# Tail rows as the stationary operand of the first expert product, transposed on TensorE, and a new order of all steps

## The chip, the core and the metric

The kernel runs on one core of a Trainium2 chip. Its engines work side by side, each through its own instructions in order: TensorE (PE: matmuls, with PEld its weight loads), VectorE (DVE), ScalarE (ACT), GpSimd (POOL, which here mostly issues DMAs), SyncE (SP, which issues DMAs). The metric is the device time of one execution in microseconds, lower is better. It is the median over several runs; a separate, profiled execution gives the trace.

## The reference

Attention with a causal window of 64 over 8 batches, 8 heads, 576 positions and head size 64; then a mixture of experts in which each batch, as a whole, is sent to one of 8 experts by the mean of its rows.

```python
scores = scale * np.matmul(q, k.transpose(0, 1, 3, 2))
mask = (rel >= 0) & (rel < window)
...
attn = attn / (np.sum(attn, axis=-1, keepdims=True) + 1e-09)
return np.matmul(attn, v).astype(np.float32)
...
pooled = x.mean(axis=1)
logits = pooled @ w_gate
e_idx = np.argmax(logits, axis=1)
...
h = np.maximum(x[mask] @ w1[e], 0.0)
out[mask] = gate_w[mask, None, None] * (h @ w2[e])
```

Per batch x is 576 x 512, w1 is 512 x 1024 and w2 1024 x 512.

## The kernel before

**Rows.** The 576 positions of a batch are 512 main rows and 64 tail rows. Attention is cut in units: four a batch with two heads each for the main rows, and a fifth for the tail rows of all heads. So unit 5b+i is part i of batch b, and units 4, 9, 14, ... are tails.

**Steps and their order.** The kernel has no loop that sets the order. `OPS`, a table of some 900 words, lists every step, and the words are carried out one after the other; each engine then runs its own instructions in that order and waits on semaphores where data or a buffer isn't ready. A word is a letter, sometimes a letter for the engine or the PSUM pool (a: ACT, d: DVE, m: the pool of the expert chunks, b: the mask is added by PE), and a number. `Q`, `t`, `L`, `W` issue loads on POOL's queue (q and k of a batch, its tail q and k, a piece of v, half of an expert's w1 or w2). `T` transposes q and k of a unit on PE, `U` and `k` copy the results out of PSUM, `S` makes the scores, `E` the exponentials, `K` masks them on DVE, `l` the row sums (spread over partitions by a matmul with ones, into the PSUM tile `lb`), `n` and `R` their Ln and the exponential of its negative on ACT (the reciprocal), `A` the product with v, `X` the scaling, with a sum over rows for the gate. `V` copies v to a second alignment (a shift by 64 partitions). `g j G H I P` work out the gate; `P` makes POOL read the expert's number, on which the addresses of the `W` loads depend.

**Expert chunks.** `c` takes the next chunk of a fixed list: in each batch eight chunks of the first product (128 hidden units by 512 main rows, 8 matmuls each), one for the tail rows, four pairs of half chunks of the second product (one pair for 128 output rows), and one for the tail's second product. `r` evacuates the oldest finished chunk on ACT (`ra`) or DVE (`rd`): a relu with the gate's weight for the first product (L446 on ACT, L448 on DVE), a copy for the second (L482, L487 for the tail). `O` and `o` store a finished output tile through POOL's or SP's queue (L492). `F` would issue filler matmuls; the table before has none.

**The tail's first product (L470).** For each of 8 tiles of 128 hidden units, 4 contraction blocks and 2 halves of 64 columns, the weights are stationary (64 columns) and the 64 tail rows are the moving operand: 64 matmuls a batch. Their result has hidden units on partitions, as the second product needs it.

**Buffers.** PSUM has eight banks: one for transposes (`ps_t`), two for scores (`ps_s`), one for `lb` and one for `av` (`ps_a`), three that expert chunks share with some transposes, scores and av (`ps_m`). V has three buffers, w1 and w2 three slots. POOL's loads and stores have eight completion semaphores in turn, so that each waits for the landing of the one eight before it.

## Time and profile before

| | |
|---|---|
| median of 3 runs | 204.0 us (203.14 to 204.12) |
| span of the profiled execution, first to last instruction | 201.9 us |
| PE busy, share of the span | 183.5 us, 91% |
| ACT, DVE, POOL busy | 131.8, 119.9, 111.0 us |
| read from and written to HBM | 61.88 and 9.44 MB |
| matmuls of the tail's first product (L470) | 512, busy 9.5 us |
| matmuls of the tail's second product (L512) | 128, busy 8.5 us |

The span of the trace and the runs' times are different measurements; what a reading of the trace gives is a difference of spans. PE's busy time counts overlapping matmuls once. The chain of waits follows the work that ended last back from the end; a piece of it on PE is the pace of successive matmuls, while the mean of a group is one matmul's own duration, longer because neighbours overlap. A wait names what came last by the profile.

### The profile page before, as it was taken

The page shows a single profiled execution, that of the slowest core. Times are in us where ns is not written, and L with a number is a line of the kernel's source. Part 1 is how long each engine was busy: PE and PEld are TensorE (multiplying, and loading weights), DVE is VectorE, ACT ScalarE, POOL GpSimd, SP SyncE. Part 2 cuts the span into 40 slices and gives each one's busy share as a digit, 9 for nine tenths or more (in the row PEclk, how much of TensorE's full clock was granted, in tenths as well). Part 3 has the DMA queues.
Part 4 walks back from the last instruction along what each step waited for, and adds up shares of the span by engine and source line. Part 5 has one row for each costly group of instructions (what it writes and reads, how often), then busy time and mean ns, then how long its engine had stood idle before and what let it go on. Part 6 is the DMA issues. An engine that isn't in the chain of part 4 may idle for free.

```text
span 201.9 us, 8105 instructions
## 1 busy us (share of the span) xinstructions
PE 183.5 (91%) x3518; PEld 124.2 (62%) x3522; DVE 119.9 (59%) x347; ACT 131.8 (65%) x247; POOL 111.0 (55%) x158
## 2 busy tenths in 40 slices
PE   0487886899999999999999999999999999999991
PEld 0455564656677756577667666676656666776760
DVE  3527989595477546895877457966494651216410
ACT  2179998876599578977779975757787436321121
POOL 7985939235931593478633552439452716553561
PEclk9999999999999999999999999999999999999998
DMA  6999999999999999999999999999999999999693
GB/s 135 175 188 159 194 162 198 199 198 174 196 201 197 170 198 193 174 201 167 200 206 200 169 195 223 259 208 137 183 237 243 266 254 212 274 212 301 235 325 134
DMA packets 83346, 41.16 MB, mean 204 GB/s; under 512 B 48080, under 2 KB 80976, under 8 KB 83312
## 3 DMA queue, kind: packets, MB, share of 16 engines
q0 software_dynamic: 81936, 39.72, 138.5%
q1 hardware_dynamic: 768, 0.85, 1.3%
q8 instruction: 27, 0.44, 0.8%
q10 hardware_dynamic: 608, 0.08, 0.2%
q14 instruction: 7, 0.06, 0.1%
HBM read 61.88 MB, written 9.44 MB: 353 GB/s over the span
## 4 chain that ended last, share of the span: by engine, by line
PE 77%; DMA 9%; POOL 7%; issue 3%; DVE 2%; ACT 1%; POOLq 0%; DVEq 0%; ACTq 0%
PE ph L461 28%; PE po L503 25%; DMA vw<-in_v_dram 9%; PE tp L225 5%; PE ph L470 4%; PE s L275 4%; PE av L331 3%; PE po L512 3%; PE lb L309 3%; POOL vw L141 2%; POOL km L110 2%; POOL qm L110 1%; POOL out_dram L492 1%; PE gps L392 1%; POOL qkt L133 1%
## 5 line engine op out<-in xcount | busy, mean ns | idle before, releaser
L503 PE MATMUL po<-w2b,hm 128*64 128x512 f16 x512 | 60.1, 379 | 0.0
L461 PE MATMUL ph<-xm,w1b 128*64 128x512 f16 x512 | 60.0, 379 | 0.0
L461 PEld LDWEIGHTS <-w1b 128*64 128x64 f16 x512 | 31.7, 110 | 18.7 <-issue 0.4
L503 PEld LDWEIGHTS <-hm 128*64 128x64 f16 x512 | 30.1, 110 | 19.3
L141 POOL DMA_DIRECT2D vw<-in_v_dram x32 | 28.9, 910 | 13.3 <-DMA w1b<-in_moe_w_dram 4.3
L446 ACT ACTIVATE hm<-ph,gw 128x512 f16<-128x512 f32 x39 | 26.6, 693 | 13.4 <-PE ph L461 13.3
L492 POOL DMA_DIRECT2D out_dram<-ob x31 | 17.2, 557 | 25.0 <-DMA w1b<-in_moe_w_dram 7.0
L351 ACT ACTIVATE ln<-lb 128x512 f32<-128x512 f32 (+1 forms) x40 | 22.5, 563 | 11.8 <-PE lb L309 8.6
L364 DVE CUSTOM_DVE_ANT_0 xm<-av,rl 128x512 f16<-128x512 f32 x32 | 21.6, 686 | 10.4 <-PE av L331 9.5
L482 ACT COPY ob<-po 128x512 f32<-128x512 f32 x18 | 10.6, 586 | 23.6 <-PE po L503 23.6
L448 DVE TENSOR_SCALAR hm<-ph,gw 128x512 f16<-128x512 f32 x25 | 18.7, 748 | 12.1 <-PE ph L461 11.6
L357 ACT ACTIVATE rl<-ln 128x512 f32<-128x512 f32 (+1 forms) x40 | 23.3, 594 | 1.5 <-DVE pool L364 1.3
L225 PE MATMUL tp<-ident,qm 128*64 128x128 bf16 x256 | 13.8, 232 | 7.4 <-DMA qm<-in_q_dram 6.9
L288 ACT ACTIVATE pe<-s 128x1024 f16<-128x1024 f32 x19 | 19.5, 1028 | 1.4 <-PE s L275 0.7
L297 DVE TENSOR_TENSOR pe<-pe,mask 128x1024 f16<-128x1024 f16 x24 | 16.3, 687 | 3.9 <-ACT pe L288 3.1
L252 ACT COPY kT<-tp 128x512 bf16<-128x512 bf16 x19 | 11.2, 597 | 9.0 <-PE tp L225 8.0
L225 PEld LDWEIGHTS <-qm 128*64 128x64 bf16 x256 | 10.7, 118 | 10.0 <-DMA qm<-in_q_dram 6.9
L482 DVE COPY ob<-po 128x512 f32<-128x512 f32 x14 | 9.7, 690 | 10.7 <-PE po L503 10.5
L423 POOL DMA_DIRECT2D w1b<-in_moe_w_dram x16 | 12.6, 785 | 5.9 <-DMA vw<-in_v_dram 2.9
L275 PEld LDWEIGHTS <-kT 64*128 64x128 bf16 x576 | 10.1, 95 | 8.9 <-issue 5.6
L331 PEld LDWEIGHTS <-vw 128*64 128x64 f16 x512 | 12.4, 112 | 4.7 <-issue 1.2
L225 PE MATMUL tp<-ident,km 128*64 128x128 bf16 x256 | 13.9, 231 | 1.4 <-DMA km<-in_k_dram 0.9
(80 smaller groups left out, 267.2 us busy)
## 6 DMA issues: line engine op xcount, KB each, us to landing
w1b<-in_moe_w_dram POOLq DMA_DIRECT2D x16, 512.0 KB, 9.3
w2b<-in_moe_w_dram POOLq DMA_DIRECT2D x16, 512.0 KB, 13.4
out_dram<-ob POOLq DMA_DIRECT2D x31, 256.0 KB, 8.1
vw<-in_v_dram POOLq DMA_DIRECT2D x32, 128.0 KB, 9.0
km<-in_k_dram POOLq DMA_DIRECT2D x7, 512.0 KB, 9.3
qm<-in_q_dram POOLq DMA_DIRECT2D x7, 512.0 KB, 9.0
out_dram<-obt POOLq DMA_DIRECT2D x14, 64.0 KB, 7.7
qkt<-in_q_dram POOLq DMA_DIRECT2D x8, 64.0 KB, 7.6
```

The costliest lines, as they stand in the source:

```text
L141: nc.gpsimd.dma_start(out=vt[:, 2 * J + 1], in_=v[b, :, 128 * J:128 * J + 128].rearrange("h c d -> c h d"))
L225: nc.tensor.transpose(tp[p0:p0 + 64, n, r], t[:, 2 * i + hh, ts(r, 64)], ident)
L288: nc.scalar.activation(out=po, in_=sp[0], func=AF.Exp, scale=scale)
L351: nc.scalar.activation(out=ln, in_=lb[:, 0:n], func=AF.Ln)
L357: nc.scalar.activation(out=rl, in_=lns.pop((b, i)), func=AF.Exp, scale=-1.0)
L364: nc.vector.tensor_tensor_reduce(out=xm[:, i], in0=av.rearrange("q r p -> q (r p)"), in1=rl, scale=1.0, scalar=0.0, op0=ALU.mult, op1=ALU.add,
L446: nc.scalar.activation(out=o, in_=i, func=AF.Relu, scale=g)
L448: nc.vector.tensor_scalar(out=o, in0=i, scalar1=g, scalar2=0.0, op0=ALU.mult, op1=ALU.max)
L461: nc.tensor.matmul(out=ph[64 * c:64 * c + 64], lhsT=w1t[:, kb, ts(2 * ft + c, 64)], rhs=xm[:, kb], start=(kb == 0), stop=(kb == 3), skip_g ...
L482: copy(e)(out=ob, in_=po)
L492: (nc.scalar if n and eng is nc.sync else eng).dma_start(out=dst, in_=src)
L503: nc.tensor.matmul(out=po[64 * c:64 * c + 64], lhsT=hm[:, fb, ts(2 * r + c, 64)], rhs=w2t[:, fb], start=(fb == 0), stop=(fb == 7), skip_gr ...
```

## The change

The 64 tail rows become the stationary operand (`xt`, 64 columns) and half of w1's columns, 512 of them, the moving one: 8 matmuls a batch. The result has rows on partitions (row half c holds hidden units 512c to 512c+511), so after the relu, now into `hs`, eight transposes on PE turn it (step `B`, into a bank of `ps_t` or, with m, `ps_m`), and a copy out of PSUM puts it into `ht` (step `D`, on ACT or DVE). The second product is as before. A 16-bit identity `identh` is copied once, in `tail_mask`. The filler matmul writes 64 partitions instead of 128, and the table uses it once, with 2 matmuls, behind the last chunk.

```diff
     def tail_mask():
+        nc.vector.tensor_copy(out=identh, in_=ident)
...
-            hts[b] = (hpool.tile([128, 8, SM], FP16, tag="hm", name="hm"),
-                      hpool.tile([128, 8, 64], FP16, tag="ht", name="ht"))
+            hts[b] = (hpool.tile([128, 8, SM], FP16, tag="hm", name="hm"), None)
...
-            ph8 = ph.rearrange("q (f t) -> q f t", f=8)
-            for f in range(8):
-                for kb in range(4):
-                    for c in range(2):
-                        nc.tensor.matmul(out=ph8[64 * c:64 * c + 64, f],
-                                         lhsT=w1t[:, kb, ts(2 * f + c, 64)], rhs=xt[:, kb],
-                                         start=(f == 0 and kb == 0), stop=(kb == 3),
-                                         skip_group_check=True)
-            evac.append(lambda e: relu(ht, ph8, gates[b], e))
+            for kb in range(4):
+                for c in range(2):
+                    nc.tensor.matmul(out=ph[64 * c:64 * c + 64], lhsT=xt[:, kb],
+                                     rhs=w1t[:, kb, ts(c, F // 2)], start=(kb == 0), stop=(kb == 3),
+                                     skip_group_check=True)
+            hss[b] = hpool.tile([128, 512], FP16, tag="hs", name="hs")
+            evac.append(lambda e: relu(hss[b], ph, gates[b], e))
+
+    def tail_tp(b, e):
+        if 'm' in e:
+            tp = ps_m.tile([128, 4, 128], FP16, tag="mo", name="htp")
+        else:
+            tp = ps_t.tile([128, 4, 128], FP16, tag="tp", name="htp")
+        for f in range(4):
+            for c in range(2):
+                nc.tensor.transpose(tp[64 * c:64 * c + 64, f], hss[b][:, ts(2 * f + c, 64)], identh)
+        htp[b] = tp
+
+    def tail_h(b, e):
+        ht = hpool.tile([128, 8, 64], FP16, tag="ht", name="ht")
+        copy(e)(out=ht.rearrange("q (c f) t -> q c f t", c=2),
+                in_=htp[b].rearrange("q f (c t) -> q c f t", c=2))
+        hts[b] = (hts[b][0], ht)
...
-                    nc.tensor.matmul(out=wps, lhsT=warm[:, 0:128], rhs=warm, start=True, stop=True)
+                    nc.tensor.matmul(out=wps[0:64], lhsT=warm[:, 0:64], rhs=warm, start=True, stop=True)
```

The table is new throughout; its last words before and now (the work of the last batch):

```diff
-    "rd O c c ra O O c c c c ra rd o O c ra O c ra o "
+    "ra c rd c O rd O o Bm7 c c c c ra Da7 c ra F2 ra o o o "
```

In the table before, 9 score steps add their mask on PE (8 main units, 1 tail), now 8 (6 main, 2 tail). Before the first `c` the table before has the steps A9 and l10, the new one doesn't, but has l14 there. Three places of the new order follow. Line numbers are one to eighteen higher in the changed program.

POOL's queue around the first expert weights (w1b_96 and w2b_99 are batch 0's slots; vw_92, vw_93, vw_91 hold v of batches 1, 2 and 3; eidx is the read of the expert's number). Before:

```order
L110 DMA km<-in_k_dram 128x8x256
L413 TENSOR_LOAD eidx
L423 ISA
L423 DMA w1b_96<-in_moe_w_dram 128x4x512
L141 DMA vw_93<-in_v_dram 128x8x64
L423 DMA w1b_96<-in_moe_w_dram 128x4x512
L426 ISA
L426 DMA w2b_99<-in_moe_w_dram 128x4x512
L141 DMA vw_93<-in_v_dram 128x8x64
```

Now:

```order
L110 DMA km<-in_k_dram 128x8x256
L415 TENSOR_LOAD eidx
L425 ISA
L425 DMA w1b_96<-in_moe_w_dram 128x4x512
L145 DMA vw_92<-in_v_dram 64x8x64
L141 DMA vw_93<-in_v_dram 128x8x64
L425 DMA w1b_96<-in_moe_w_dram 128x4x512
L141 DMA vw_93<-in_v_dram 128x8x64 x3
L428 DMA w2b_99<-in_moe_w_dram 128x4x512
L141 DMA vw_91<-in_v_dram 128x8x64 x4
```

All four main pieces of batch 2's v now stand ahead of the w2 loads, batch 1's v tail behind the first half of w1, and batch 3's v comes next.

ACT ahead of the first relu of an expert chunk (ln and rl are the steps n and R, pe and pp the exponentials of a main and of a tail unit, kT, qt and qtt copies out of PSUM). Before:

```order
L288 ACTIVATE pe<-s 128x1024
L357 ACTIVATE rl<-ln 128x512
L351 ACTIVATE ln<-lb 128x512
L291 ACTIVATE pp<-s 128x256 x2
L351 ACTIVATE ln<-lb 128x256
L291 ACTIVATE pe<-s 128x512 x2
L252 COPY kT_95<-tp 128x512
L357 ACTIVATE rl<-ln 128x256
L446 ACTIVATE hm<-ph,gw 128x512
```

Now:

```order
L353 ACTIVATE ln<-lb 128x512
L257 COPY kT_94<-tpt 128x4x64
L359 ACTIVATE rl<-ln 128x512
L248 COPY qtt<-tpt 128x256
L290 ACTIVATE pe<-s 128x1024
L293 ACTIVATE pp<-s 128x256 x2
L353 ACTIVATE ln<-lb 128x256
L359 ACTIVATE rl<-ln 128x256
L254 COPY kT_95<-tp 128x512
L448 ACTIVATE hm<-ph,gw 128x512
```

The two copies of batch 2's tail now lie on ACT in this stretch, and two short Ln (units 9 and 14) stand in it instead of one.

DVE around the gate of batch 1 and the V shift of batch 2 (vw_93; gmx and eidx are the gate's maximum and the expert's number). Before:

```order
L448 TENSOR_SCALAR hm<-ph,gw 128x512
L403 MAX gmx<-gps 128x8
L404 MAX_INDEX eidx<-gmx,gps 128x8
L407 TENSOR_SCALAR gnm<-gmx 128x1
L297 TENSOR_TENSOR pe<-pe,mask 128x1024
L448 TENSOR_SCALAR ht<-ph,gw 128x512
L150 COPY vw_93<-vw_93 64x4x512
L151 COPY vw_93<-vw_93 64x4x512
```

Now:

```order
L386 TENSOR_REDUCE grd<-gpr 128x8
L299 TENSOR_TENSOR pe<-pe,mask 128x1024
L150 COPY vw_93<-vw_93 64x4x512
L151 COPY vw_93<-vw_93 64x4x512
L450 TENSOR_SCALAR hm<-ph,gw 128x512
L405 MAX gmx<-gps 128x8
L406 MAX_INDEX eidx<-gmx,gps 128x8
L409 TENSOR_SCALAR gnm<-gmx 128x1
L450 TENSOR_SCALAR hs<-ph,gw 128x512
```

The shift now comes ahead of a relu, of the gate and of the tail's relu; before it came behind all three.

More of the change, by code (lines that the diff above doesn't have):

```diff
@@ L157 @@
     ident = const.tile([128, 128], BF16)
+    identh = const.tile([128, 128], FP16)
     mb = const.tile([128, 4, 16], FP16)
@@ L465, in w1_chunk @@
         else:
[L466 to L474 removed]
+            for kb in range(4):
[5 more added lines that the diff above has]
+            evac.append(lambda e: relu(hss[b], ph, gates[b], e))
+    hss = {}
+    htp = {}
+    def tail_tp(b, e):
[12 more added lines that the diff above has]
+        hts[b] = (hts[b][0], ht)
     pos = {}
@@ L530 @@
     unit_eops = {"T": unit_tp, "U": unit_q, "k": unit_kt, "S": unit_s, "A": unit_a}
+    tail_ops = {"B": tail_tp, "D": tail_h}
     batch_ops = {"g": gate0, "j": gate_mm, "G": gate1, "H": gate_w, "I": gate2, "V": shift_v,
@@ L557 @@
                 load_qk(int(x.split(".")[0]), x.partition(".")[2])
+            elif c in tail_ops:
+                tail_ops[c](int(x), e)
             elif c in batch_ops:
```

68 rows, old and new, of the table OPS are left out of this document.

## The prediction

> **What bounds the kernel now.** I read the page first, then the busy time by stretch, TensorE's waits, and the chain of waits in order of time. The page:
>
> ```profile
> span 201.9 us, 8105 instructions
> PE 183.5 (91%) x3518; PEld 124.2 (62%) x3522; DVE 119.9 (59%) x347; ACT 131.8 (65%) x247; POOL 111.0 (55%) x158
> PEclk9999999999999999999999999999999999999998
> ```
>
> TensorE (PE) is busy for 91% at the full granted clock. Where are the other 18 us? In the windows the columns are the stretch, its length, then busy us of PE, weight loads, DVE, ACT, POOL, the clock, the DMA share and GB/s:
>
> ```profile
> 20.50:41.00 20.50, 15.92 (x463) 11.81 (x466) 16.61 (x51) 18.66 (x38) 13.57 (x18) 1.00 1.67 189
> 41.00:197.60 156.60, 156.50 (x2838) 104.57 (x2832) 94.15 (x268) 101.97 (x193) 80.94 (x115) 1.00 1.40 213
> 197.60:201.90 4.30, 0.01 (x1) 0.00 (x0) 0.00 (x0) 0.37 (x1) 0.54 (x1) 0.81 0.33 112
> ```
>
> From 41.0 to 197.6 PE is idle for 0.1 us in 156.6: there the time is PE's own work, and no cheaper ACT, DVE or POOL step shortens it. Ahead of 41 PE idles 4.6 us in the second half of the opening, behind loads and behind ACT, which is 91% busy there (18.66 of 20.50). The last 4.3 us are evacuation, stores and the closing barrier. So the time is: when the expert chunks begin, plus the PE work left then, plus 4.3. The first chunk starts here:
>
> ```profile
> 40.84 4.48 PE L461 MATMUL ph<-xm,w1b 128*64 128x512 f16 x40
> L423 POOL DMA_DIRECT2D w1b<-in_moe_w_dram x2: 752/796/839, 30.0 to 31.7; - x2
> DMA to landing us min/median/max: 9.4/10.3/11.2
> ```
>
> The first half of batch 0's w1 is issued at 30.0 and lands 9.4 later, at 39.4, so the first chunk came 1.4 us after its weights: attention work ahead of it in PE's order held it.
>
> **The tail product.** Pieces of the chain (start, us, what), in which successive matmuls overlap, so that they are the pace and not the latency:
>
> ```profile
> 39.06 0.12 PE al L339 x8
> 40.09 0.22 PE lb L309 x2
> 40.31 0.25 PE av L331 x16
> 40.56 0.45 PE tp L225 x16
> 47.63 0.11 PE lb L314 x2
> 47.74 0.86 PE ph L461 x8
> 48.60 1.01 PE ph L470 x64
> 55.77 0.23 PE tpt L232 x8
> ```
>
> Removed in each batch: 64 small matmuls, 1.01 us. Added: 8 matmuls with 512 moving columns in two column halves, the form of an ordinary chunk, 0.86; and 8 transposes of a 64-column stationary against 128 columns, the form of L232 x8, 0.23. Sum +0.08 a batch, +0.6 in eight. The instructions fall from 64 to 16, but PE's time does not fall with them: the old matmuls ran at 1.01 / 64 = 16 ns. From below I find nothing under 0.86 + 0.23; from above, half of a short group such as lb (0.11) lost at a change of form adds 0.9 to the eight, giving +1.5. I take +0.6, the rows of the same shapes.
>
> [...]
>
> Also added per batch: one PSUM copy of 128x512. The nearest row for it, the row of a single transpose, and the row of the relus on VectorE (count | busy us, mean ns of one):
>
> ```profile
> L252 ACT COPY kT<-tp 128x512 bf16<-128x512 bf16 x19 | 11.2, 597 | 9.0 <-PE tp L225 8.0 <-DVE qt L242 0.9
> L232 PE MATMUL tpt<-ident,qkt 128*64 128x128 bf16 x64 | 3.2, 221 | 0.0
> L448 DVE TENSOR_SCALAR hm<-ph,gw 128x512 f16<-128x512 f32 x25 | 18.7, 748 | 12.1 <-PE ph L461 11.6
> ```
>
> The copy is 0.6 us, 5 us in all, on engines that idle a third or more of the stretch after 41 (ACT 102 of 156.6 busy, DVE 94). Cost nothing: in the tightest batch, the last, four half chunks (4 x 0.86 = 3.4) stand on PE between the transposes and the tail's second product; ACT evacuates row 2 from 1.7 on (0.6), then copies (0.6), done at 2.9. Without that cover it is 0.6 a batch. The two filler matmuls at the very end are 2 x 0.11 us of array time (0.86 / 8 each), beside the last evacuation and the stores; without that cover, 0.2. The 0.1 us copy of the identity lies in the opening, under the first loads.
>
> **The work left at the first chunk.** Of attention work before it, the new order leaves out A9 and l10 (0.12 + 0.22) and adds l14 (0.11): 0.23 more remains. The masks moved onto PE (two main units fewer, one tail more) all lie before the first chunk, under its waits; they count nothing. So PE has 0.6 + 0.2 = 0.8 us more to do after its first chunk.
>
> **When the first chunk starts.** Every POOL load goes through one queue, in order. In POOL's new order 64 KB fewer stand ahead of the first w1 half (batch 1's V tail moved behind it): 64 KB at the 189 GB/s of the windows is 0.3 us, so it lands at 39.1. The batch-1 V loads also come 0.3 earlier. Their shift and what follows:
>
> ```profile
> 31.32 0.88 DVE vw L150
> 32.22 0.76 DVE vw L151
> ```
>
> Shift from 31.0 to 32.7; then on PE av 0.25, transposes 0.45, lb 0.22: ACT can take that lb's Ln at 33.6. From there the new order has on ACT, up to the Ln that frees the lb bank for l14, PE's last step before the chunk: four 512-wide Ln or Exp (L351 twice, L357 twice), a kT tail copy, a qtt copy, two wide Exp (L288), two halves of L291 and a short Ln:
>
> ```profile
> L357 ACT ACTIVATE rl<-ln 128x512 f32<-128x512 f32 x32 | 20.2, 638 | 1.5 <-DVE pool L364 1.3
> L288 ACT ACTIVATE pe<-s 128x1024 f16<-128x1024 f32 x19 | 19.5, 1028 | 1.4 <-PE s L275 0.7 <-PE av L331 0.5
> L351 ACT ACTIVATE ln<-lb 128x512 f32<-128x512 f32 x32 | 19.4, 606 | 9.4 <-PE lb L309 8.6 <-PE av L331 0.6
> L246 ACT COPY qtt<-tpt 128x256 bf16<-128x256 bf16 x2 | 0.7, 353 | 0.0
> L291 ACT ACTIVATE pp<-s 128x256 f16<-128x256 f32 x6 | 2.0, 381 | 0.1
> L351 ACT ACTIVATE ln<-lb 128x256 f32<-128x256 f32 x8 | 3.1, 390 | 2.5 <-PE lb L314 2.5
> ```
>
> 2 x 0.61 + 2 x 0.64 + 2 x 1.03 + 2 x 0.35 (both copies have L246's shape) + 2 x 0.38 + 0.39 = 6.4 us end to end. Neighbours may overlap (PE's groups do); with 0.1 for each of the ten it is 5.4. So that Ln ends at 39.0 to 40.0, and the chunk, 0.1 after, falls at 39.1 to 40.1. The low bound is the weights' landing, 39.1; the high one 41.0, if ACT waits in this stretch as it did before:
>
> ```profile
> 34.79 0.63 ACT L357 ACTIVATE rl<-ln 128x512 f32<-128x512 f32 x1 [0.31 <-DVE pool L364]
> 40.44 0.60 ACT L351 ACTIVATE ln<-lb 128x512 f32<-128x512 f32 x1 [0.62 <-PE av L331]
> ```
>
> I take 39.8, nearer the end-to-end sum because ACT did wait before: 1.0 earlier than 40.84.
>
> **The end.** Row 3 moves from POOL's queue to SP's. The last rows before:
>
> ```profile
> 197.65 0.54 POOL L492 DMA_DIRECT2D out_dram<-ob  x1 [1.07 <-ACT ob L482]
> 198.05 0.56 ACTq L492 DMA_DIRECT2D out_dram<-obt  x1
> ```
>
> Both were issued within 0.5 us of each other; without the POOL one the ACT-issued half row still ends the program. I take -0.1, between 0 and -0.4 (the gap in issue).
>
> **Sum.** -1.0 + 0.8 - 0.1 = -0.3: a profiled span of 201.6 for 201.9. The runs shown lie 2.1 above the span (204.0 against 201.9), which I keep: 203.7. With the bounds of the parts it reaches from -1.7 + 0.8 - 0.4 = -1.3 to +0.2 + 1.7 + 0 = +1.9, 202.7 to 205.9. A difference under 0.5%, 1.0 us, can't be told from none here.
>
> **Rivals.** (a) Slower: VectorE parks at the V shift of batch 2. In the new order that shift stands ahead of a relu and of batch 1's routing; before it came behind them, and even so
>
> ```profile
> 51.04 0.69 DVE L150 COPY vw<-vw 64x2048 f16<-64x2048 f16 x1 [0.63 <-DMA qkt<-in_q_dram]
> L141 POOL DMA_DIRECT2D vw<-in_v_dram x4: 886/934/1015, 19.8 to 22.7; - x4
> DMA to landing us min/median/max: 8.2/8.3/8.5
> ```
>
> it waited for transfers. Four such loads, landing 0.7 (128 KB at 189 GB/s) to 1.1 apart (8.5 + 22.7 - 8.2 - 19.8, by 3), and one w1 half (512 KB, 2.8) now follow the first w1 half's 39.1, with a V tail of 0.3: the last lands at 45.0 to 46.6. Shift (0.69 + 0.76) and relu (0.75) end at 47.2 to 48.8. PE needs that relu's bank for an av after nine chunks (7.8) and l10, A9, l11, scores and gate (1.0): 39.8 + 8.8 = 48.6. So there is 1.4 us of cover, or none; past that each us late is a us lost, and routing, and with it batch 1's weights behind it on POOL, is late by the same. With one w1 half more in the loads' way (2.8) against the middle of the cover (0.7), 2.1 are lost: 205.8. It decides from 0.7 late. For it: the wait above. Against: PE shows no wait of any kind after 41, so such plans have held so far.
>
> (b) Faster: the first chunk starts as soon as its weights are there, 39.1: -1.7 + 0.8 - 0.2 = -1.1, 202.9. For it: 1.4 us of slack before. Against: ACT, 91% busy, is in front of it.
>
> (c) Slower: the clock falls, or rises later, in the opening, where the order of first loads changed.
>
> ```profile
> 9.26 0.64 PE L225 MATMUL tp<-ident,km 128*64 128x128 bf16 x8
> 17.53 0.39 PE L225 MATMUL tp<-ident,qm 128*64 128x128 bf16 x8
> 12.90:20.20 7.30, 6.01 (x144) 3.96 (x142) 3.99 (x10) 6.85 (x13) 4.56 (x7) 1.00 2.08 170
> PE av L331 <- DVE pool L364: 1.1, 1, 1.1
> ```
>
> Eight transposes took 0.64 at 9.3 and 0.39 at 17.5: 0.25 more for what paces at 0.22, so about half speed at first. PE is busy 6.0 us between 12.9 and 20.2; at half speed that needs up to 6.0 more, of which the idle 1.3 there and 2.7 of the 4.6 later absorb 4.0. The first chunk 2 us later: 205.7. PE's longest wait once it has begun is the 1.1 of the last row, and its clock row stays at 9 (even at 9.3, where the paces say otherwise, so that row can't settle it): I give this little. [...]
>
> (d) The new transposes don't overlap, and each takes the 221 ns of L232's row by itself: 64 x (0.22 - 0.03) = 12 us more, 216. Every quoted group of transposes denies it. [...]
>
> **How the numbers follow.** Forecast (within 1.0 us of 204.0) 0.45; (a) 0.27; (b) 0.19; (c) 0.08; (d) 0.01. Faster is (b), 0.19; slower is (a), (c) and (d), 0.36. The range, 202.5 to 206.0, holds the bounds of the sum and (a), (b), (c); the forecast's own is 203.0 to 205.0.
>
> **What would show it.** Tail chunk 0.86 and transposes 0.23 on the chain; first chunk at 39.8; no PE wait after it; the end 4.2 us after PE's last product. A first chunk later than 41, a DVE wait at L150 above 1.5 us near 46, or a clock under 1.00 between 13 and 41 would make the forecast wrong.

## The result, and the profile after

The changed kernel takes 212.67 us (median of 4 runs, 211.38 to 212.97), the kernel before on the same chip 203.71 (203.14 to 204.12): 1.043 times as long, with a 95% interval of 1.039 to 1.047. The forecast was 203.7 in a range of 202.5 to 206.0. The profiled execution's own time is 212.97, its span 211.4 against 201.9. Executions of one kernel below differ by 3 to 5 us in several cases, and by more in two, and the clock granted to TensorE falls in some of them and not in others (its mean is 0.979 to 0.999 over the four executions with both routings earlier); stages are therefore compared on profiled executions, one for each kernel.

The page of the changed kernel, then its windows (columns as in the prediction):

```profile
span 211.4 us, 7337 instructions
...
PE 188.9 (89%) x3138; PEld 117.5 (56%) x3138; DVE 132.0 (62%) x369; ACT 124.4 (59%) x230; POOL 111.3 (53%) x156
...
PEclk9995899999999999999999999999999999999998
...
q8 instruction: 24, 0.39, 0.7%
...
PE 59%; DMA 15%; DVE 7%; POOL 6%; issue 5%; ACT 4%; POOLq 1%; DVEq 0%; ACTq 0%
```

```profile
12.00:15.50 3.50, 1.67 (x43) 1.10 (x42) 1.69 (x5) 2.54 (x5) 2.95 (x4) 1.00 1.70 184
15.50:22.30 6.80, 6.33 (x86) 3.47 (x82) 3.63 (x7) 5.33 (x12) 5.44 (x7) 0.50 1.95 176
...
43.70:130.40 86.70, 86.22 (x1466) 53.78 (x1464) 66.39 (x189) 58.66 (x107) 43.04 (x54) 1.00 1.55 186
130.40:206.00 75.60, 73.24 (x1004) 43.90 (x998) 39.14 (x102) 37.09 (x70) 37.30 (x59) 1.00 1.07 216
206.00:211.40 5.40, 0.00 (x0) 0.00 (x0) 0.00 (x0) 0.00 (x0) 0.00 (x0) 0.87 0.69 223
```

The same stages of the kernel before (130.4 here and 126.0 there are the starts of batch 4's first chunk):

```profile
12.00:15.50 3.50, 2.90 (x63) 1.57 (x62) 0.75 (x3) 2.77 (x6) 2.26 (x4) 1.00 1.68 187
...
40.80:126.00 85.20, 85.20 (x1698) 56.34 (x1693) 58.31 (x174) 65.94 (x126) 44.50 (x57) 1.00 1.60 192
126.00:197.60 71.60, 71.50 (x1150) 48.38 (x1150) 36.05 (x94) 36.22 (x68) 36.64 (x59) 1.00 1.15 239
```

So the 9.5 us of span went to four places: the first chunk at 43.7 for 40.8 (+2.8), 86.7 for 85.2 up to batch 4 (+1.5), 75.6 for 71.6 to PE's end (+4.0), and 5.4 for 4.3 behind it (+1.1). From the first chunk to PE's end PE is busy for 159.46 us in place of 156.70 and idle for 2.84 in place of 0.10: half of the loss there is waiting, the other half is busy time. TensorE's waits (us in total, times, longest) name only the first half and a part of the opening's loss:

```profile
PE tp L227 <- DMA qm<-in_q_dram: 8.7, 3, 7.0
PE tp L227 <- issue: 1.9, 1, 1.9
PE ph L462 <- DMA w1b<-in_moe_w_dram: 1.2, 1, 1.2
PE po L521 <- DMA w2b<-in_moe_w_dram: 1.0, 1, 1.0
```

The rows of the kernel before for the first two; it has no wait for weights:

```profile
PE tp L225 <- DMA qm<-in_q_dram: 6.9, 1, 6.9
...
PE tp L225 <- issue: 0.5, 1, 0.5
```

**Opening.** PE waits 1.3 us at 13.3 to 14.5 for the queries of heads 0 and 1, whose load the new order puts behind others. It is busy for 1.67 us of the window from 12.0 to 15.5 (2.90 before), and from 15.5 to 22.3 the granted clock is 0.50. Near 39.6 PE stops for 1.9 us in the middle of eight transposes, and the profile names nothing that it waits for (`issue`):

```profile
39.07 0.39 PE L227 MATMUL tp<-ident,qm 128*64 128x128 bf16 x8
39.29 0.33 PE L227 MATMUL tp<-ident,km 128*64 128x128 bf16 x5
41.55 0.27 PE L227 MATMUL tp<-ident,km 128*64 128x128 bf16 x3 [1.92 <-issue]
```

**Second half.** The chain of waits (start, us, what) runs through the routing of batch 6, POOL, and two weight loads:

```profile
156.93 0.18 DVE gmx L405
...
157.13 0.24 DVE eidx L406 x2
...
159.00 0.55 POOL w1b L425
...
163.02 8.84 DMA w1b<-in_moe_w_dram
...
171.91 1.05 PE ph L462 x8
...
184.94 13.27 DMA w2b<-in_moe_w_dram
...
198.25 2.78 PE po L521 x24
201.03 0.22 PE htp L485 x8
```

The argmax of batch 6 (gmx, eidx) is ready at 157.4. The load issued at 163.02, which PE then waits for, is the first half of w1 (`W24`): the new order puts it behind the second half (`W25`, at 159.00), four stores and a load of v, while the kernel before issues the first half first, at 149.50. POOL stands at the read of the argmax until it is ready; its timeline, with the idle time ahead in brackets, first for batch 1 and then for batch 6, and the row of batch 1 of the kernel before (the name in a bracket is the last release that the profile sees, for batch 6 not the argmax that the chain shows):

```profile
53.50 0.69 POOL L133 DMA_DIRECT2D qkt<-in_q_dram  x1 [6.64 <-DVE gnm L409]
...
158.34 0.57 POOL L510 DMA_DIRECT2D out_dram<-ob  x1 [10.52 <-DVE pe L299]
```

```profile
47.65 0.88 POOL L110 DMA_DIRECT2D qm<-in_q_dram  x1 [3.89 <-PE ph L461]
```

While POOL stands, it puts nothing into its DMA queue: in two windows of the same twelve microseconds, before and after, it has 9 instructions and 2, and the DMA moves 242 and 167 GB/s (the last column):

```profile
146.00:158.00 12.00, 11.98 (x257) 7.63 (x252) 7.93 (x21) 10.29 (x20) 5.32 (x9) 1.00 1.22 242
```

```profile
146.00:158.00 12.00, 12.00 (x198) 7.63 (x196) 7.56 (x29) 7.95 (x17) 1.45 (x2) 1.00 1.14 167
```

From the DMA packets of the traces, MB moved by a time:

| | 60 us | 150 | 160 | 170 | 190 |
|---|---|---|---|---|---|
| before | 10.91 | 28.47 | 30.99 | 33.45 | 38.43 |
| changed | 10.09 | 27.64 | 28.97 | 30.84 | 35.57 |

The queue falls 0.8 MB behind near 50 to 60 us and 1.2 more near 150 to 160.

### The profile page after: what moved, and what is told of

Its sections match the earlier page's. It is cut to its first block, busy times and chain, and to the rows that moved or that the text cites. A ratio compares the mean times of both kernels' runs of the same rounds, so it can differ in the third digit from the quotient of the medians.

```text
span 211.4 us, 7337 instructions
## 1 busy us (share of the span) xinstructions
PE 188.9 (89%) x3138; PEld 117.5 (56%) x3138; DVE 132.0 (62%) x369; ACT 124.4 (59%) x230; POOL 111.3 (53%) x156
## 4 chain that ended last, share of the span: by engine, by line
PE 59%; DMA 15%; DVE 7%; POOL 6%; issue 5%; ACT 4%; POOLq 1%; DVEq 0%; ACTq 0%
PE po L521 19%; PE ph L462 16%; DMA w2b<-in_moe_w_dram 6%; PE tp L227 5%; DMA qm<-in_q_dram 4%; PE s L277 4%; DMA w1b<-in_moe_w_dram 4%; PE av L333 3%; PE po L530 2%; PE lb L311 2%; PE ph L469 2%; DVE hm L450 2%; POOL out_dram L510 2%; ACT pe L290 2%; DVE xm L366 1%
## 5 line engine op out<-in xcount | busy, mean ns | idle before, releaser
L462 PEld LDWEIGHTS <-w1b 128*64 128x64 f16 x512 | 28.6, 110 | 21.7 <-DMA w1b<-in_moe_w_dram 1.5
L521 PEld LDWEIGHTS <-hm 128*64 128x64 f16 x512 | 28.4, 110 | 21.8 <-issue 1.3
L450 DVE TENSOR_SCALAR hm<-ph,gw 128x512 f16<-128x512 f32 x36 | 26.8, 746 | 14.0 <-PE ph L462 13.7
L510 POOL DMA_DIRECT2D out_dram<-ob x29 | 16.1, 557 | 31.1 <-DVE pe L299 10.5
L448 ACT ACTIVATE hm<-ph,gw 128x512 f16<-128x512 f32 x28 | 19.1, 690 | 18.3 <-PE ph L462 17.9
L290 ACT ACTIVATE pe<-s 128x1024 f16<-128x1024 f32 x25 | 25.8, 1031 | 1.8 <-PE av L333 1.2
L500 ACT COPY ob<-po 128x512 f32<-128x512 f32 x16 | 9.4, 586 | 19.8 <-PE po L521 19.8
L299 DVE TENSOR_TENSOR pe<-pe,mask 128x1024 f16<-128x1024 f16 x26 | 17.7, 685 | 2.8 <-ACT pe L293 2.6
L500 DVE COPY ob<-po 128x512 f32<-128x512 f32 x16 | 11.0, 690 | 13.3 <-PE po L521 13.3
L428 POOL DMA_DIRECT2D w2b<-in_moe_w_dram x16 | 12.4, 783 | 8.1 <-DMA w1b<-in_moe_w_dram 5.0
L254 DVE COPY kT<-tp 128x512 bf16<-128x512 bf16 x18 | 12.1, 683 | 5.9 <-PE tp L227 5.9
```

The lines of the kernel that those rows point to most:

```text
L290: nc.scalar.activation(out=po, in_=sp[0], func=AF.Exp, scale=scale)
L450: nc.vector.tensor_scalar(out=o, in0=i, scalar1=g, scalar2=0.0, op0=ALU.mult, op1=ALU.max)
L462: nc.tensor.matmul(out=ph[64 * c:64 * c + 64], lhsT=w1t[:, kb, ts(2 * ft + c, 64)], rhs=xm[:, kb], start=(kb == 0), stop=(kb == 3), skip_g ...
L500: copy(e)(out=ob, in_=po)
L510: (nc.scalar if n and eng is nc.sync else eng).dma_start(out=dst, in_=src)
L521: nc.tensor.matmul(out=po[64 * c:64 * c + 64], lhsT=hm[:, fb, ts(2 * r + c, 64)], rhs=w2t[:, fb], start=(fb == 0), stop=(fb == 7), skip_gr ...
```

## The experiments

Times are medians; the kernel before ran beside each group (203.65, 204.00, 204.03, 203.65 and 203.91 us). Words of the step table are shown as diffs against the changed kernel where nothing else is said.

### Old product, new order

The tail's product as before (64 small matmuls, no transposes), in the new order, without the two filler matmuls at the end.

```diff
-c l13 B0 A11 S18 I1
+c l13 A11 S18 I1
...
-c c Da0 E15 ra
+c c E15 ra
```

> The new order with the old tail product (64 small matmuls, no transposes, no extra copy, no filler at the end). If the order alone makes the loss: the clock falls as before in the opening and the span is 210.3 to 211.4 us (0 to 1 us less than 211.4, eight times the 0.08 to 0.13 us that the new tail costs on TensorE). If the new tail product makes it (its copy and transposes hold up the chunks' banks): 202 to 206 us.

Measured: 221.1 us (218.0, 220.2, 222.1, 228.3), slower than either kernel and outside both expectations. Five stalls like the one near 39.6 cost 7.1 us in all, besides a shorter one in an expert chunk:

```profile
PE av L331 <- issue: 5.5, 4, 2.2
PE tp L225 <- issue: 1.6, 1, 1.6
```

So in the new order the old product brings stalls of its own, and the run does not show what the order costs alone. The count of PE's instructions at two of these stalls stands in a table below.

### New product, old order

Against the kernel before, with its product changed; the transposes into the bank of the attention's transposes, the copy right behind them:

```diff
-c V2 Ua16 c c ra ka16 l11 A10
+c V2 Ua16 c c ra ka16 B0 Da0 l11 A10
```

> The old order with the new tail product; transposes and copy are put in one after the other, at least two chunks after the tail's relu, each copy on the engine that did not do that relu. If the order makes the loss: span 202.3 to 203.4 us, 0.5 to 1.5 above the 201.9 of the kernel before. If the new tail product makes it: 206 us or more.

Measured: 207.67 (207.27 to 208.25), 1.020 [1.016, 1.023], with a span of 205.8 between the two theories. New waits:

```profile
PE gps L395 <- DVE grd L387: 0.9, 1, 0.9
PE tp L228 <- ACT ht L491: 0.7, 1, 0.7
...
PE tp L228 <- DVE ht L491: 0.3, 1, 0.3
```

The next unit's transposes (L228) wait 0.7 and 0.3 us for the copy out of the shared bank (L491). With another place for both:

```diff
-c V2 Ua16 c c ra ka16 l11 A10 X10 Am12 W4 c Q9
+c V2 Ua16 c Bm0 c ra ka16 l11 A10 X10 Am12 W4 c Da0 Q9
```

> The order of the kernel before with the new tail product, as in the run with the old order, but the transposed tail goes to a bank of the expert chunks' pool in place of the attention's transposes, and its copy stands two chunks behind it. Theory A (the new tail itself costs 0.08 us a batch, and the 4 us of the earlier run were waits for the shared bank and for an engine parked at a copy): 204.2 to 205.2, and no wait of PE for the copied tail. Theory B (the copies themselves overload ACT and DVE, or the tail's product holds PE longer than its rows say): 206.3 to 208.

Measured: 205.25 (204.44 to 205.64, 10 runs), 1.0047 [1.0025, 1.0069]. No wait for the copied tail is left: theory A, at the upper end of its range. So the tail product by itself costs about 1.0 to 1.3 us, and 7.4 us (212.67 less 205.25) come with the new order. Behind the first chunk PE is busy for 157.6 us here and idle for 1.0. The tail product's rows:

```profile
L470 PE MATMUL ph<-w1b,xt 128*64 128x512 f16 x64 | 8.3, 380 | 0.0
...
L486 PE MATMUL htp<-identh,hs 128*64 128x128 f16 x64 | 3.2, 220 | 0.4 <-ACT pe L294 0.4
```

### Which half of the new order loses

Both with the new product. The seam lies at the next to last chunk of batch 3; first the old order up to there and the new one behind it:

```diff
 l30 c X29 X25 rd ka31 g5 c
-O K33 rd Sm31 n30 S34 j5 G5 c
+Ud31 ra c n30 ra c K33 S31 c ra E31 c j5 G5
```

> The order of the kernel before (with the new tail, as in the run of 205.25 us) up to the next to last expert chunk of batch 3, then the new order for all that is left. Theory A (the new order loses in two places that don't depend on each other: 2.8 to 3.7 us in the opening, and about 4 in the last batches through late weights and stores that bunch): 208.4 to 210. Theory B (what the new order loses is a lateness of the DMA queue that begins in its first batches and is never made up): with the old first half the queue is on time, and the time is 205.3 to 207.

and the reverse:

```diff
 c X29 c E32 rd Dd3 K32 R25 ra
-Ud31 ra c n30 ra c K33 S31 c
+Am25 W18 W19 X25 g5 O O O c O K33 rd Sm31 n30 S34 j5 G5 c
```

> The reverse: the new order up to the next to last expert chunk of batch 3, then the order of the kernel before. Theory A (losses by place): the opening's loss stays and that of the last batches goes: 208 to 209.7. Theory B (the queue's lateness is carried on): 211 to 213, with waits for weights or stores in the last batches although their order is the old one.

Measured: 207.90 (207.54 to 208.62), 1.021 [1.017, 1.025], and 208.90 (208.16 to 211.17), 1.028 [1.021, 1.036]. Over the 205.25 of the old order with the new product, the second half loses 2.65 and the first 3.65; together 6.3 of 7.4. The first fell between the theories, the second where theory A had it. The stages of the profiled executions:

| | first chunk | to batch 4 | to PE's end | behind it | span |
|---|---|---|---|---|---|
| before | 40.8 | 85.2 | 71.6 | 4.3 | 201.9 |
| old order, new product | 41.2 | 86.3 | 72.3 | 4.3 | 204.0 |
| old, then new order | 40.6 | 85.4 | 75.2 | 4.8 | 205.9 |
| new, then old order | 42.1 | 88.5 | 72.0 | 4.1 | 206.7 |
| changed kernel | 43.7 | 86.7 | 75.6 | 5.4 | 211.4 |

The new second half takes 75 us and the old one 72, whichever first half stands ahead; a lateness handed down from the opening would not do that. Part of the 3 us is work and not delay: at batch 4's first chunk the new order still has 24 score, 16 av and 4 gate matmuls ahead of it that the old order has done by then, an estimated 0.9 us by the paces of such groups in these traces (0.34 and 0.22 for the scores, 0.25, 0.10). The 88.5 of the new, then old order includes them. In the run with the old first half the queue was on time at 150 us (28.75 MB), moved 0.75 MB in the next ten, and the weights of batch 6 came late:

```profile
PE ph L463 <- DMA w1b<-in_moe_w_dram: 1.8, 1, 1.8
```

### The second half: routing, weights, stores

The weights of batches 6 and 7 ahead of stores (only the piece of batch 6 is shown):

```diff
-P6 O Ua39 ra H6 W25 O ra rd K38
+P6 W24 W25 Ua39 ra H6 O O ra rd K38
...
-c ra W24 W26 W27 O O I6
+c ra W27 O O O I6
```

> The changed kernel with the loads of the weights of batches 6 and 7 issued ahead of the stores that stood between them, and both halves of the first weights of batch 6 right behind its routing. Theory A (late weights): the waits of 1.2 us at the first chunk of batch 6 and of 1.0 us in batch 7 are gone or under 0.3, PE ends 1.8 to 2.3 us earlier and the time is 209.6 to 210.9. Theory B (the DMA queue is full there, and what goes ahead only pushes other transfers back): the stores land later, the time from PE's last product to the end grows by as much as PE gained, and the time is 211.8 to 213.

Measured: 216.3 (213.2, 214.5, 218.0, 218.2). Both waits for weights are gone, and two for output buffers stand in their place, PE's waits for copies into `ob` and `obt`. That these copies stand behind older stores from the same buffers is the author's reading; the chain runs through a store of `obt` for 4% of the span (`DMA out_dram<-obt`):

```profile
PE ph L463 <- ACT obt L506: 2.7, 1, 2.7
PE po L522 <- ACT ob L501: 2.1, 1, 2.1
```

Theory B, and dearer than it said. The run shows one thing more: POOL stands at the read of batch 6's routing for as long as in the changed kernel (10.5 us), and yet, with both halves of w1 issued right behind it (at 156.58), no wait for them is left. Instead, the routing of batch 6 earlier, the order of loads and stores as it is:

```diff
-c g6 I5 L36 ra c c j6 rd c W22 O K37 rd c G6 L37 K36 P6
+c g6 I5 L36 ra j6 G6 c c rd c W22 O K37 rd c L37 K36 P6
```

> The changed kernel with the routing of batch 6 earlier: its product with the gate stands two expert chunks earlier on PE and its argmax right behind that, ahead of the copies that stood between. Theory A (late routing makes the weights of batch 6 late): POOL issues the first weights of batch 6 at 1.5 to 2.5 us earlier against the chunks, the wait of 1.2 us at the first chunk of batch 6 falls under 0.4, and the time is 210.8 to 211.7. Theory B (the queue is full, and it is the stores and loads in front of the weights that count): the wait stays within 0.4 us or goes over to a wait for an output buffer, and the time is 212.2 to 213.2.

Measured: 210.87 (208.42, 210.02, 211.71, 212.13), 1.036 [1.029, 1.043], 1.8 less than the changed kernel, though the intervals touch. In the profiled execution, the shortest of the four, POOL passes the read at 154.27 for 158.34, no wait for weights is left in either batch, and the stage that took 75.6 is

```profile
128.00:201.30 73.30, 73.16 (x1006) 44.32 (x1002) 39.19 (x102) 37.18 (x71) 36.81 (x59) 1.00 1.11 224
```

Theory A. The mirror image, late routing put into the old order with the new product:

```diff
-E38 j6 c c G6 P6 Ud39 E37 ra ra c V7 K38 rd H6 c l36 c K37 W24
+E38 c c Ud39 E37 ra ra c V7 K38 rd c j6 l36 c K37 G6 P6 H6 W24
```

> The mirror image: the old order with the new tail (205.25 us), in which only the routing of batch 6 is put later: the product with the gate three chunks later on PE, the argmax and POOL's read behind the fifth chunk of batch 5, about 5 us later than it was, as far as the new order has it. Nothing else moves. Theory A (late routing alone explains what the second half loses, 2.65 us by the run with the old first half): a wait of PE for the first weights of batch 6 of 1 to 2.5 us appears, the DMA queue runs dry near 150 to 158, and the time is 206.8 to 208.3. Theory B (the second half loses by its order of stores and evacuations): the old order has room for it, and the time is 204.9 to 206.0.

Measured: 206.29 (205.62 to 208.17), 1.0 over 205.25, between the theories. The first half of w1 was issued 2.8 us later (153.84 for 151.05), not the 5 intended, 14.5 us ahead of its first chunk, and still came in time. What cost was another wait: the gate's product shares its bank with `lb`, and ACT's read of it (gex) had moved too.

```profile
PE lb L312 <- ACT gex L435: 1.4, 1, 1.4
```

So this run does not go as far as the changed kernel, where the first half is issued 8.9 us ahead of its chunk. By this and the two runs before it, the late weights take both: routing that is late, and a first half that the order puts behind the second half and stores. Earlier routing alone removes the waits for them, and so does the first half right behind the read.

### The opening: clock, loads, instructions

Filler matmuls on zeros where PE waits, to hold the clock:

```diff
-L1 L3 Tm0 l3
+L1 L3 f6 Tm0 l3
...
+            elif c == "f":
+                wps = ps_a.tile([128, 512], FP32, tag="av", name="wpf")
+                for _ in range(int(x)):
+                    nc.tensor.matmul(out=wps[0:64], lhsT=warm[:, 0:64], rhs=warm, start=True, stop=True)
```

(one more ahead of S2, three ahead of T5)

> The changed kernel with ten filler matmuls of 512 columns on TensorE in its opening (1 ahead of the scores of unit 2, 6 ahead of the transposes of unit 0, 3 ahead of those of unit 5), written to the idle av bank. Theory A (the clock fell because TensorE stood idle from 13.3 to 14.5 us, and that delayed the opening): the granted clock stays at 1.00 after 12 us, the first expert chunk starts at 41 to 42 us instead of 43.7, and the span is 209 to 210 us instead of 211.4. Theory B (the opening is set by loads and ScalarE; half speed there is covered): the first chunk stays within 0.5 us of 43.7 and the span within 1 us of 211.4, whatever the clock does.

Measured: 213.88 (213.14 to 216.15), 1.052 [1.044, 1.059], outside both theories; the first chunk came at 44.6. The clock held through the loads, at 1.00, and fell at the stall near 39 instead, to 0.51:

```profile
15.50:22.30 6.80, 6.23 (x133) 3.67 (x130) 3.83 (x7) 6.64 (x14) 5.66 (x8) 1.00 1.95 176
...
39.00:45.90 6.90, 5.68 (x89) 4.65 (x90) 2.81 (x6) 2.81 (x7) 3.92 (x6) 0.51 1.77 185
```

The old opening with the new order behind it (the seam is put together by hand):

```diff
 kd15 ka17 T16 K14 L11 c
-Ud18 kd18 n14 l10 Am9 ka15 L13 Ud15 I0 c L12 R14 ra c
+n10 l14 X8 R9 c n14 E13 R14 ra c X9 L10 c
```

> The old order up to the first expert chunk, then the new order (with the new tail). If the loss is spread over the opening (2.8 us), weights that come late for batches 6 and 7 (2.7 us) and the end (1.5 us): the first chunk starts at 40.8 us, the span is 207.5 to 209 us, and the late weights of batches 6 and 7 stay. If all of it follows from the late start: 202 to 204 us and no wait for weights. If the opening is not it: 210.5 us or more.

Measured: 213.79 (211.74 to 214.88), 1.050 [1.047, 1.053]. The first chunk came at 40.6, but the seam made VectorE wait at the shift of batch 2's v, and PE 2.5 us for a relu behind it. The time is in the range that was to mean that the opening is not it, but with that loss at the seam it says nothing on the opening; the run with the seam at batch 3 took its place.

The first two loads put back:

```diff
-Q0.48 i Q1.48 Y0.24 Cd0.24 Y1.24 y Q3 t0 Q1.2 Q0.2 L0
+Q0.48 i Q1.48 Q0.2 Y0.24 Cd0.24 Y1.24 y Q1.2 Q3 t0 L0
```

> The changed kernel with two of its first loads put back where the kernel before has them: the query and key of heads 0 and 1 of batch 0 are issued ahead of the tail of batch 0 and of the first part of batch 1. Theory A (the opening lost time through its loads and the clock that fell on the gap): PE's 1.3 us wait for the query of heads 0 and 1 near 13.3 to 14.5 is gone, no record at 0.5 begins near 15.5, the first expert chunk starts at 41.5 to 42.6 in place of 43.7, and the time is 210.6 to 211.6. Theory B (the wait only passes to the next load, and the refill of PE's instructions sets the first chunk): first chunk at 43.2 or later, time 212.0 to 213.0.

Measured: 211.81 (209.90 to 212.93), 1.036 [1.029, 1.044]. The 1.3 us wait is gone and PE is 1.8 us further at 37.0, but it stalls for 1.6 us with nothing named (`issue`), the clock falls there (0.50 from 39.0 to 42.5) and the first chunk starts at 43.0: of 1.8 us 0.7 is left.

Two units' transposes behind the first chunk:

```diff
-R8 Tm18 l9 E11 n9 L11 W1 Tm15 S13 l14 kd17 R9 Ud17 K10 c Ud18 kd18 n14 l10 Am9 ka15
+R8 l9 E11 n9 L11 W1 S13 l14 kd17 R9 Ud17 K10 c Tm18 Ud18 kd18 n14 l10 Am9 Tm15 ka15
```

> The changed kernel with the transposes of unit 18 and unit 15 moved from before the first expert chunk to behind it; nothing else. Theory A (PE's 1.9 us without an instruction at 39.6 to 41.6 is a refill of its instructions, which short matmuls in a row use up faster than it comes): the stall shrinks under 0.8 us, the first chunk starts at 41.5 or earlier (1.0 us of transposes moved and 1.1 or more of the stall), and the time is 211.0 to 211.8. Theory B (the stall belongs to a wait for a buffer or a copy that the profile doesn't name): it stays at 1.5 us or more in front of the same transposes, the first chunk starts near 42.7, and the time stays at 212.2 to 213.2.

Measured: 213.66 (211.95, 212.32, 215.01, 215.36), 1.051 [1.043, 1.059]. The stall fell to 0.8 and the first chunk came at 41.4, as theory A has it, but the time did not follow: the transposes stand in the chunks' banks, and the second chunk waits for their copies.

```profile
43.98 0.41 PE L228 MATMUL tp<-ident,qm 128*64 128x128 bf16 x8 [0.78 <-DVE kT L255]
...
45.76 0.59 PE L463 MATMUL ph<-xm,w1b 128*64 128x512 f16 x3 [1.14 <-DVE qt L245]
```

Forty small matmuls ahead of all of PE's work:

```diff
-Q0.48 i Q1.48 Y0.24
+f40 Q0.48 i Q1.48 Y0.24
...
+            elif c == "f":
+                wps = ps_a.tile([128, 512], FP32, tag="av", name="wpf")
+                for _ in range(int(x)):
+                    nc.tensor.matmul(out=wps[0:64, 0:16], lhsT=warm[:, 0:64], rhs=warm[:, 0:16], start=True, stop=True)
```

> The changed kernel with 40 matmuls of 16 columns on zeros ahead of all of PE's work, in the time in which PE waits for its first load; they shift the count of PE's instructions by 80 and cost no time there. If PE's stall of 1.9 us near 39.6 to 41.6 is a refill of instructions at a fixed count (every 256, at 189 over a multiple in all runs so far), it comes at the same count again, and so 40 matmuls earlier in the program's order, ahead of the transposes of unit 17 or in front of their first ones, and the transposes that it stood in front of run through. If it is a wait that belongs to those transposes (a bank, a copy, a load), it stays in front of the same ones.

Measured, a single execution: 211.43; in its opening the clock was at half for 3.4 us in place of 6.8, so that what counts is the place of the stall and not the time. All transposes run through, the first chunk comes at 41.30, and the stall stands behind it:

```profile
41.30 1.03 PE L463 MATMUL ph<-xm,w1b 128*64 128x512 f16 x8
...
42.38 0.29 PE L342 MATMUL al<-pp,vw 128*64 128x64 f16 x7
44.22 0.19 PE L342 MATMUL al<-pp,vw 128*64 128x64 f16 x1 [1.55 <-issue]
```

It did not come 40 matmuls earlier, as expected (at that count PE had just been idle 0.6 us for ACT, and stopped for 0.1), but at a count 252 higher (1469 for 1217). So the stall did not stay with the transposes; what recurs is the count, taken over multiples of 256. Counting PE's matmuls, weight loads and semaphore instructions up to where it goes on, with the start of the 16,384-byte packet on the queue `q8 instruction` that came just before:

| kernel | packet starts | PE goes on | after | count | over a multiple of 256 |
|---|---|---|---|---|---|
| before | 36.23 | 38.68 | 2.45 | 1213 | 189 |
| changed | 39.19 | 41.55 | 2.36 | 1217 | 193 |
| old product, new order | 99.16 | 101.49 | 2.33 | 3517 | 189 |
| the same | 148.38 | 150.70 | 2.32 | 5309 | 189 |
| two units' transposes later | 37.74 | 39.96 | 2.22 | 1213 | 189 |
| forty matmuls ahead | 41.95 | 44.22 | 2.27 | 1469 | 189 |

### Reads of the routing later, and mends together

POOL's read of batch 1's routing behind loads that don't need it:

```diff
-L14 P1 t3 n13 E18
+L14 t3 Q8 Q9 P1 n13 E18
```

> The changed kernel with POOL's read of batch 1's routing moved behind three groups of loads that don't need it (the tail of batch 2, and query and key of batch 2's partner batch), so that the DMA queue has work while POOL waits for the routing. Theory B (the 0.8 MB that the queue falls behind near 50 to 60 us is carried to the end): bytes moved by 60 us rise from 10.1 to 10.6 MB or more, the waits for weights in the last batches shrink, and the time is 210 to 211.6. Theory A (the last batches are late through their own routing and order): bytes by 60 us rise, but the time stays at 212 to 213.2 and the two waits for weights stay within 0.3 us.

Measured: 211.82 (three of four runs at 211.2 to 212, one at 249.2), 1.038 [1.033, 1.043]. By 60 us 10.64 MB had moved, but at 160 us it was 29.10, as little as in the changed kernel. 0.9 us less, between the theories; the wait for batch 6's weights stayed (1.1), that of batch 7 fell to 0.3, and a new one of 0.6 came at batch 1's. That the edit made the 0.9 is not shown: the intervals overlap, and the clock was at half for 3.4 us in place of 6.8 in the profiled execution.

Three mends at once: the forty matmuls, this one and the earlier routing of batch 6.

> The changed kernel with three mends at once: the 40 small matmuls ahead of PE's work, the read of batch 1's routing behind loads that don't need it, and the earlier routing of batch 6. If the losses stand in places that don't depend on each other, the single gains add (0.9 by the later read, about 1.2 by each of the others) and the time is 208.6 to 210. If a full DMA queue takes back what is won, it is 210.5 to 212.

Measured: 210.38 (209.85, 210.32, 210.44, 213.88), 1.031 [1.024, 1.038], between the two. The first chunk came at 40.0, yet the first chunk of batch 1 at 63.9, as in the run with the later read alone, behind a wait for batch 1's weights:

```profile
PE ph L463 <- DMA w1b<-in_moe_w_dram: 1.4, 1, 1.4
```

So the routing of batch 1 as well, in place of the later read:

```diff
-V2 j1 ra c c ra ka16 rd c Am10 A12 Ua16 ra G1
+V2 j1 G1 ra c c ra ka16 rd c Am10 A12 Ua16 ra
...
-L14 P1 t3 n13
+L14 P1 W4 W5 t3 n13
```

> As the run with three mends, but the routing of batch 1 is mended as that of batch 6 was: its argmax stands right behind its product with the gate, POOL's read stays where the changed kernel has it, and the first weights of batch 1 are issued right behind it, ahead of the loads of batch 2. In the run with three mends PE's first chunk came at 40.0 but the first chunk of batch 1 at 63.9, with a wait of 1.4 us for its weights. Theory A (once the opening is mended, the late routing of batch 1 sets the time): those weights are issued at 49 to 50.5 in place of 52.9, the first chunk of batch 1 starts at 61.5 to 62.8, and the time is 208.3 to 209.6. Theory B (other transfers that are pushed back by these take the place): the first chunk of batch 1 moves by less than 0.7 or a wait for query, key or values appears behind it, and the time is 210 to 211.5.

Measured: 211.03 (209.20, 209.28, 212.78, 213.32): two executions are shorter than all four with the three mends and two are longer than three of them, so the times decide nothing. In the profiled execution (span 207.7 for 208.7) theory A held in its details: the weights were issued at 49.3, their wait went to 0.3 us, and batch 1's first chunk came at 62.6 in place of 63.9. But PE's waits from 41 to 70 us are now

```profile
PE al L342 <- issue: 1.5, 1, 1.5
PE tpt L235 <- DMA qkt<-in_k_dram: 0.7, 1, 0.7
```

The first is a stall with nothing named, like the one near 39.6; the second is a load that the weights pushed back, as theory B has it. No run beat the kernel before, and none points to a version that would; of all with the new product the one in the old order is the fastest.

## Why the prediction was wrong

In spans the forecast was -1.0 us for the first chunk, +0.8 for PE's work behind it, nothing for waits there and -0.1 for the end. Measured are +2.8, +2.8, +2.7 and +1.1.

**The tail product: right.** The new chunk paces at 0.86 and the transposes at 0.22, and the old order with the new product loses 1.0 to 1.3 us where +0.6 was taken and +1.5 was the bound.

**The copy costs nothing: right for the changed kernel**, where no wait names it, but the reason was too narrow. The run with the shared bank shows what the sentence left out: the next transposes wait for the copy out of it, 0.7 us at the longest. The copy of the identity, 0.1 us in the forecast, took 0.36, and no wait names it.

**PE's work behind the first chunk, +0.8: mis-sized, +2.8.** The product makes 0.9 of it (157.6 us busy in the old order, 156.7 before). The other 1.9 come with the new order and no wait names them: the two fillers end 0.4 us behind the last product, and the rest is spread over groups of short matmuls. Why these take longer stays open. The term of 0.23 for work left at the first chunk can't be seen beside this.

**First chunk at 39.8: wrong, 43.7.** The weights landed at 39.26 where 39.1 was forecast, so the queue's sum held. The step that failed is the start of ACT's chain: the forecast put the shift of v at 31.0 and the Ln behind it at 33.6; the trace has 32.93 and 35.82. From there to the end of the chain's last Ln it took 7.4 us, of which 2.0 are a wait for PE that the forecast doesn't have:

```profile
42.86 0.38 ACT L353 ACTIVATE ln<-lb 128x256 f32<-128x256 f32 x1 [1.99 <-PE lb L316]
```

Without that wait it is 5.4, the overlapped sum and not the 6.4 that was taken. So the forecast took the opening's pace and clock for given, and PE for never stopping. Three things lay outside it: a 1.3 us wait for a load moved back (gone when put back), the clock at half for 6.8 us (rival (c), priced at +2 and given 0.08), and a stall of 1.9 us with nothing named, against 0.5 before. How much of it is the clock, five profiled executions with the same words up to the first chunk bound: it came at 41.9 and 42.4 with no fall, at 41.5 and 42.3 with one of 3.4 us, and at 42.1 with half speed up to 17.6 and no fall, each with a stall of 1.0 to 1.6 us with nothing named. By these the long fall cost an estimated 1.3 to 2.2 (43.7 less 42.4 and 41.5), a longer stall among it, and without any fall the chunk is still 2 us late or more. In the last run, where the stall stands behind the first chunk, no load holds PE by more than 0.7 us after the first one, and the clock, up late at 16.5, does not fall, the shift began at 31.01, the Ln at 33.93 and the first chunk at 39.6: the forecast's steps hold where nothing else steps in.

**"From 41.0 to 197.6 PE is idle for 0.1 us ... there the time is PE's own work": wrong when carried over to the new order.** This step put the waits at nothing; PE idles 2.8 us, 2.2 of them for weights of batches 6 and 7. The cover over the loads belonged to the old order. The forecast compared the order in POOL's queue around the first weights only. What counts is when POOL gets to a load: it stands at the read of the routing, for 10.5 us at batch 6, and then has the second half of w1 and stores ahead of the first half. Earlier routing removes both waits for weights, and so do the weights right behind the read (shown by the two runs); that the routing is late because the new order puts the last attention units of batch 6 further back among the chunks is read from the chain, not tried by itself.

**The end, -0.1: wrong, +1.1.** In the last 5.4 us the DMA moves 223 GB/s, against 112 before: more is left to store. Late weights are not needed for that, since with earlier routing and no wait for weights it is still 5.5; with the old second half it is 4.1. Which of the moved stores makes it was not tried.

**Rivals.** (a) did not happen as told: the shift ran at 48.77 with no wait. Its last clause, routing late and weights late with it, is what happened at batch 6, from another cause. (b) and (d) are out. (c) happened, as part of the opening's 2.8. Each rival was one event priced alone; none had several small delays at once, and the upper bound came from the largest of them.

What stays open: about 1 us that the two halves' losses don't add up to, the 1.9 us of PE's busy time, the end, and the share of the first half that lies in the clock, which falls in one execution and not in the next.

## What to carry to other kernels

A middle without waits shows that loads are covered by this order, not that they are covered: before an order is changed, list for each load when its queue's engine will reach it (what that engine stands at ahead of it included, as POOL did for 10.5 us at the read of batch 6's routing) and when it is used. Where PE and the DMA are both nearly full (in the changed kernel PE is busy for 89% of the span, and the DMA engines for 90% or more in 33 of its 40 slices), a mend of one wait can be taken back by the next (of 1.8 us in the opening 0.7 was left, and early weights brought waits for output buffers), so price a new order by what it makes late, not by the first difference. A new product in the place of an old one is best tried in the old order first: here that costs 0.5% and the new order 3.6%.

## What the runs showed of the hardware

**PE stopped at counts that recur.** The six stalls of the table above end at 189 to 193 over a multiple of 256 in the count of PE's instructions (1213, 1469, 3517 and 5309 are 256, 2048 and 1792 apart), and 2.2 to 2.5 us after the start of a 16,384-byte packet on the instruction queue. Stalls of 0.4 us or more with nothing named cost 0.5 us in the kernel before, 1.9 in the changed one and 7.1 with the old product in the new order, which has about as many matmuls as the kernel before (3,516 for 3,518), so that their number alone does not make it. The trace of the changed kernel has 24 such packets for 6,276 matmuls and weight loads, 262 to a packet; that of the kernel before has 27 for 7,040, 261 to a packet. That PE waits for its instructions there is the author's reading of count and packet; no row of the profile names it. In the changed kernel the stall stands among transposes that follow one another at 28 ns (0.45 us for 16).

**The clock fell with no wait of PE longer than 1.3 us ahead of it.** In the changed kernel it is at 0.50 from 15.48 to 22.31 us. In the 3.42 us ahead of that PE is busy for 1.59, 46%, and its longest wait is 1.3. From 39.38 to 42.79, over the stall of 1.9 us, PE is busy for 1.49 of 3.41 us, 44%, and the clock stays at 1.00, so the busy share alone does not decide. With the fillers PE is busy for 2.58 us from 12.0 to 15.5, where the changed kernel has 1.67, and the clock stays at 1.00 up to 39.0. What makes it fall is not shown.
